# Attention and MoE in one kernel: batch 1's attention in another order, and the last output tile by column halves

## Chip, cores, metric

One core of one Trainium2 chip. The metric is device time in microseconds. The kernel before takes 328.93 us (median of 3 runs, 327.4 to 330.0). With one core there is no other core to compare with, so a run is marked slow here when it is over 1.5% above the fastest of the same kernel. Engines: PE is TensorE (PEld its weight loads), ACT the scalar engine, DVE VectorE, POOL GpSimd, SP the sync engine; a "q" behind the name (SPq) is the engine's sequencer.

## The reference, cut to what matters

```python
# q, k, v: (batch 8, heads 8, seq 576, head_dim 64), f32
scores = q @ k.transpose / sqrt(64)
heads 0..3: mask rel in [0, 32)            # "local"
heads 4..7: mask same position modulo 32   # "strided"
x = softmax(scores) @ v                    # -> (4608 tokens, 512)
h = x @ w_in                               # layer 1: 512 -> 2048
g = where(h > 0, h, exp(min(h, 0)) - 1)
out = g @ w_out                            # layer 2: 2048 -> 512
```

## The kernel before

The order in which each engine works is written by hand; every engine takes its own queue in order. Tokens go through the MoE in 18 groups of 256; `l2` is a quarter of a layer 2 tile (four matmuls of 512 columns, 0.87 us), used as filler for TensorE wherever attention leaves it waiting. While batch 1's attention runs, a string of tokens says what stands next: "2" one layer 2 step, S scores, A or B the product P v (A in a two-bank PSUM tile, B in two one-bank tiles), E the normalisation, T transposes, "a" casts of K and V, "c" the cast of K's second half, "v" loads of batch 2's V, "k" and "x" further loads, "t" transposes of batch 2. The tiles that the timelines name: `sc` scores, `pm` the masked weights, `so` or `o_ps` with `s_ps` the product P v and its sums, `ln` and `rc` the normalisation, `tp` transposes, `xT` attention's output as layer 1 reads it, `hps` layer 1, `ops` and `opl` layer 2, `osb` the output tile in SBUF, `qlb` and `klb` the local heads' Q and K in bf16, `vlx` and `vs` the V of the local and of the strided heads.

```python
p_x = tile_pool("ps_x", bufs=2)   # PSUM, two banks each: scores, A, transposes
p_h = tile_pool("ps_h", bufs=3)   # PSUM, one bank each: layer 1, B
p_o = tile_pool("ps_o", bufs=1)   # PSUM, one bank: layer 2
...
def load_vl16(b):
    for h in range(HG):           # two loads for each of 4 heads
        ...
        nc.gpsimd.dma_start(out=t[PRE:128], in_=x)
        nc.gpsimd.dma_start(out=t[0:PRE, 1:], in_=...)
...
for it in ("2 S4 2 S5 2 2 B4 S6 2 E4 A5 S7 2 E5 B6 a 2 E6 A7 2 E7 v "
           "T0 2 S0 S1 c 2 T1 k B0 2 E0 S2 2 A1 E1 S3 2 B2 E2 2 A3 2 E3 t 2 x").split():
    if it == "2":
        l2_to(l2n[0] + 1)
    elif it == "v":
        load_str(2, vs, v)        # one load, into vs
        load_vl16(2)              # eight loads, into vlx
    elif it == "a":
        cast_k(nc.gpsimd, 0)      # klb, read by T0
        for a in range(2):
            cast_v(nc.gpsimd, 1, a)
    elif it == "c":
        cast_k(nc.scalar, 1)      # klb, read by T1
    ...
for n, (j, t) in enumerate(L1S):  # the main loop
    ...
    l2_to(n + 10)
    ...
    l1(j, t, ...)
```

The last tile's layer 2 is four such steps, one copy by the scalar engine and two stores (56 and 72 rows) by the sync engine.

The softmax here doesn't subtract the row's maximum and nothing guards it: scores larger than these inputs give would overflow.

## Time and profile before

| stage of the profiled run (span 325.9 us) | ends at |
|---|---|
| warm-up, batch 0's attention, first layer 1 | last 16 layer 1 matmuls start at 38.58 us |
| batch 1's attention with 16 layer 2 steps | 65.23 us |
| main loop | last layer 1 group starts at 314.73 us |
| last layer 2 matmul | 321.82 us |
| last copy | 322.44 us |
| end | 325.9 us |

TensorE sets the time in all of them but the end. A row of the timeline reads: start, length (us), engine, line, what it writes and reads, how many; in brackets how long the engine stood idle ahead of it and what released it. At the start of the main loop, TensorE in the kernel before:

```profile
69.97 0.31 PE L359 MATMUL so<-pm,ones 72*64 72x288 bf16 x2 [0.37 <-DVE pm L289]
71.57 0.31 PE L359 MATMUL so<-pm,ones 72*64 72x288 bf16 x2 [1.16 <-DVE pm L289]
72.94 0.30 PE L284 MATMUL sc<-qsT,ksT 64*128 64x72 bf16 x8
```

Two P v products wait 1.53 us together for VectorE. At the end, the DMA activity from 320 to 326 us in 40 slices of 0.15 us (tenths busy, then GB/s):

```profile
DMA  4767862100000000000002578868520000000000
GB/s 150 232 177 205 287 219 96 41 0 0 0 0 0 0 0 0 0 0 0 0 0 96 205 205 246 259 205 246 150 109 27 0 0 0 0 0 0 0 0 0
```

The last tile's data move in slices 21 to 30, 323.15 to 324.65 us; 1.25 us pass from there to the end.

### The profile page before, as it was taken

To read this page: it belongs to the slowest core of one execution; us is meant where nothing else is said; L and a number is where in the kernel's file an instruction comes from. 1 tells how busy PE (TensorE), PEld (TensorE's weight loads), DVE (VectorE), ACT (ScalarE), POOL (GpSimd) and SP (SyncE) were. 2 spreads that over 40 slices of the span, in tenths; PEclk is the share of its full clock that TensorE was granted. 3 is DMA by queue.
4 is the path that set the end of the run, shared out by engine and by line. 5 is a ranking of instruction groups with operands and counts; after the bars stand their busy time and mean duration, and the time that the engine had idled before them with its cause. 6 is when DMAs were issued, how large, how long until landed. Compare 5 with 4: busy or idle time off the path is not lost.

```text
span 325.9 us, 7664 instructions
## 1 busy us (share of the span) xinstructions
PE 309.4 (95%) x2933; PEld 222.6 (68%) x2976; DVE 246.0 (75%) x481; ACT 221.0 (68%) x429; POOL 101.2 (31%) x121
## 2 busy tenths in 40 slices
PE   8899997989999989999999999989999999999994
PEld 6669944566667767767777677757777777777762
DVE  6764973467778898898888988998888866666660
ACT  3798765687778877777778777877877734444431
POOL 6262414962672445263245443540000000000000
PEclk9999999999999999999999999999999999999999
DMA  8999999999799939992999299939111111111212
GB/s 165 192 207 209 221 185 151 141 193 184 114 126 214 202 87 146 224 183 68 132 224 217 70 144 232 174 92 162 48 45 37 34 34 32 33 34 44 55 32 64
DMA packets 55179, 41.98 MB, mean 129 GB/s; under 512 B 38296, under 2 KB 45784, under 8 KB 55144
## 3 DMA queue, kind: packets, MB, share of 16 engines
q0 software_dynamic: 21040, 24.49, 45.7%
q1 hardware_dynamic: 32780, 16.42, 24.6%
q10 hardware_dynamic: 1324, 0.59, 0.8%
q8 instruction: 23, 0.38, 0.5%
q14 instruction: 12, 0.10, 0.1%
HBM read 38.18 MB, written 9.44 MB: 146 GB/s over the span
## 4 chain that ended last, share of the span: by engine, by line
PE 74%; DVE 13%; ACT 5%; issue 4%; DMA 3%; POOL 0%; DVEq 0%; ACTq 0%
PE ops L454 32%; PE hps L397 30%; DVE g L412 3%; PE ox L336 3%; PE sc L284 3%; DVE he L411 3%; DMA ks<-in_k_dram 3%; DVE xT L304 2%; PE idle L464 1%; DVE pm L295 1%; DVE g L431 1%; PE hpw L422 1%; DVE xT L308 1%; PE tp L261 1%; PE o_ps L369 1%
## 5 line engine op out<-in xcount | busy, mean ns | idle before, releaser
L454 PE MATMUL ops<-w_out_sb,g 128*128 128x512 bf16 x533 | 140.5, 380 | 2.7 <-issue 0.8
L397 PE MATMUL hps<-xT,w_in_sb 128*128 128x256 bf16 x1088 | 140.7, 273 | 0.6 <-DVE g L412 0.4
L397 PEld LDWEIGHTS <-w_in_sb 128*128 128x128 bf16 x1088 | 117.4, 114 | 22.7 <-issue 0.6
L404 ACT ACTIVATE he<-hps 128x512 f32<-128x512 f32 x136 | 80.2, 593 | 53.7 <-PE hps L397 52.7
L412 DVE TENSOR_TENSOR g<-he,hps 128x512 bf16<-128x512 bf16 x130 | 89.4, 687 | 13.5
L454 PEld LDWEIGHTS <-g 128*128 128x128 bf16 x576 | 52.0, 98 | 39.1 <-DVE g L412 0.3
L411 DVE TENSOR_SCALAR he<-he 128x512 bf16<-128x512 f32 x130 | 59.9, 461 | 20.5 <-ACT he L404 19.1
L287 ACT ACTIVATE e<-sc 128x576 bf16<-128x576 f32 (+1 forms) x64 | 38.6, 645 | 4.5 <-PE sc L284 4.4
L459 ACT COPY osb<-ops 128x512 f32<-128x512 f32 x36 | 21.1, 587 | 15.5 <-PE ops L454 13.2
L339 ACT ACTIVATE ln<-ox 64x288 f32<-64x288 f32 x40 | 16.3, 409 | 12.3 <-PE ox L336 11.7
L304 DVE TENSOR_TENSOR xT<-ox,rc 64x288 bf16<-64x288 f32 x40 | 18.1, 453 | 5.0 <-ACT rc L342 4.7
L308 DVE TENSOR_TENSOR xT<-ox,rc 64x288 bf16<-64x288 f32 x40 | 18.1, 453 | 4.0 <-ACT rc L342 3.7
L295 DVE TENSOR_TENSOR pm<-e,mask_l 128x576 bf16<-128x576 bf16 x32 | 17.9, 591 | 3.3 <-ACT e L287 3.0
L150 POOL COPY vsx<-vs 72x1024 bf16<-72x1024 bf16 x10 | 11.2, 1146 | 23.9 <-DMA vs<-in_v_dram 18.8
L342 ACT ACTIVATE rc<-ln 128x288 f32<-128x288 f32 x40 | 17.7, 443 | 1.3
L289 DVE TENSOR_TENSOR pm<-e,mask_s 72x576 bf16<-72x576 bf16 x32 | 16.0, 527 | 2.5 <-ACT e L287 2.2
L340 ACT ACTIVATE ln<-ox 64x288 f32<-64x288 f32 x40 | 16.1, 402 | 0.5
L464 PE MATMUL idle<-warm 128*128 128x256 bf16 x92 | 15.1, 312 | 1.3 <-DVE warm L173 1.3
L144 POOL CAST vlx<-vl 128x768 bf16<-128x768 f32 x13 | 10.6, 843 | 17.6 <-DMA vl<-in_v_dram 16.6
L138 POOL CAST klb<-kl 96x768 bf16<-96x768 f32 x11 | 9.8, 907 | 19.9 <-DMA kl<-in_k_dram 14.8
L129 POOL DMA_DIRECT2D qs<-in_q_dram x8 | 6.5, 806 | 29.9 <-DMA qsT<-qs 25.2
L135 POOL CAST qlb<-ql 72x1024 bf16<-72x1024 f32 x10 | 11.6, 1186 | 3.8 <-DMA ql<-in_q_dram 3.8
(98 smaller groups left out, 256.4 us busy)
## 6 DMA issues: line engine op xcount, KB each, us to landing
out_dram<-osb SPq DMA_DIRECT2D x32, 144.0 KB
vl<-in_v_dram POOLq DMA_DIRECT2D x7, 576.0 KB, 17.8
kl<-in_k_dram POOLq DMA_DIRECT2D x6, 576.0 KB, 14.6
ql<-in_q_dram POOLq DMA_DIRECT2D x5, 576.0 KB, 15.7
qs<-in_q_dram POOLq DMA_DIRECT2D x8, 288.0 KB, 7.4
ks<-in_k_dram POOLq DMA_DIRECT2D x8, 288.0 KB, 9.7
vs<-in_v_dram POOLq DMA_DIRECT2D x8, 288.0 KB, 9.7
w_in_sb<-in_moe_w_in_dram POOLq DMA_DIRECT2D x2, 1024.0 KB, 16.3
```

The costliest lines, as they stand in the source:

```text
L287: nc.scalar.activation(e[0:R], sc[0:R, :, 0:W], ACT.Exp, scale=scale)
L295: nc.vector.tensor_mul(pm, e, mb.unsqueeze(1).to_broadcast([128, 2, W]))
L304: nc.vector.tensor_mul(xs[:, u * W:(u + 1) * W], o[pr], rc[pr])
L308: nc.vector.tensor_mul(dst, o[pr].rearrange(pat, b=3, s=NS), rc[pr].rearrange(pat, b=3, s=NS))
L342: nc.scalar.activation(rc, ln, ACT.Exp, scale=-1.0)
L397: nc.tensor.matmul(hps[:, mm], lhsT=w_in_of(m, c), rhs=xT[:, c, r0:r0 + SUB], start=(c == 0), stop=(c == KC - 1))
L404: nc.scalar.activation(e, hps, ACT.Exp)
L411: eng.tensor_scalar(e1, e, scalar1=1.0, scalar2=1.0, op0=ALU.min, op1=ALU.subtract)
L412: nc.vector.tensor_tensor(gt, e1, hps, op=ALU.max)
L454: nc.tensor.matmul(ops, lhsT=g[:, m, kk * 128:(kk + 1) * 128], rhs=w_out_sb[:, m, :], start=(m == 0), stop=(m == MC - 1))
L459: nc.scalar.copy(o_sb, ops)
L464: nc.tensor.matmul(ps, lhsT=warm[:, 0:128], rhs=warm[:, 0:ps.shape[-1]], start=True, stop=True, skip_group_check=True)
```

## The change

Its intent: join the visits to the scores, put every P v of batch 1 in one-bank tiles so that they do not compete with the scores, move three layer 2 steps into the main loop's first iterations where TensorE waits, and let the last tile's copy and store start sooner and on two engines. On the way "v" came to stand ahead of "a", both K casts went to GpSimd, and the second copy of the first transposes (T0) went from the scalar engine to VectorE. The cut below leaves out the lines of the function `l2_to` that now call `l2_last` for the last tile.

```diff
-    def store(c0, o_sb):
+    def store(c0, o_sb, cols=slice(0, 512), engs=(nc.sync,)):
 ...
+            engs[i % len(engs)].dma_start(out=out_v[b, s, p:p + n, cols],
+                                          in_=o_sb[c - c0:c - c0 + n, cols])
+    def l2_last(j, kk):
+        for i in range(2):
+            ops = p_h.tile([128, n], F32, tag="h", name="opl")     # n = 256
+            for m in range(MC):
+                nc.tensor.matmul(ops, lhsT=..., rhs=w_out_sb[:, m, i * n:(i + 1) * n], ...)
+            nc.scalar.copy(o_sb[:, i * n:i * n + n // 2], ops[:, 0:n // 2])
+            nc.vector.tensor_copy(o_sb[:, i * n + n // 2:(i + 1) * n], ops[:, n // 2:])
+            store(j * SUB + kk * 128, o_sb, slice(i * n, (i + 1) * n), (nc.sync, nc.scalar))
 ...
-    for it in ("2 S4 2 S5 2 2 B4 S6 2 E4 A5 S7 2 E5 B6 a 2 E6 A7 2 E7 v "
-               "T0 2 S0 S1 c 2 T1 k B0 2 E0 S2 2 A1 E1 S3 2 B2 E2 2 A3 2 E3 t 2 x").split():
+    for it in ("2 S4 S5 2 2 B4 S6 S7 E4 2 B5 2 E5 B6 2 E6 B7 2 E7 v a "
+               "T0 2 S0 S1 2 T1 k B0 2 E0 S2 S3 B1 2 E1 B2 2 E2 B3 2 E3 t x").split():
 ...
         elif it == "a":
-            cast_k(nc.gpsimd, 0)
+            for a in range(2):
+                cast_k(nc.gpsimd, a)
             for a in range(2):
                 cast_v(nc.gpsimd, 1, a)
-        elif it == "c":
-            cast_k(nc.scalar, 1)
 ...
-            piece_T(1, n, (nc.vector, nc.scalar))
+            piece_T(1, n, (nc.vector, nc.scalar if n else nc.vector))
 ...
-        l2_to(n + 10)
+        l2_to(max(n + 10, min(n + 13, 16)))
```

More of the change, by code (lines that the diff above doesn't have):

```diff
@@ L434 @@
     out_v = out.rearrange("(b p s) f -> b s p f", b=B, s=NS)
-    def store(c0, o_sb):
-        c = c0
+    def store(c0, o_sb, cols=slice(0, 512), engs=(nc.sync,)):
+        c, i = c0, 0
         while c < c0 + 128:
@@ L441, in store @@
             n = min(RS - p, c0 + 128 - c)
-            nc.sync.dma_start(out=out_v[b, s, p:p + n, :],
-                              in_=o_sb[c - c0:c - c0 + n, :])
-            c += n
+            engs[i % len(engs)].dma_start(out=out_v[b, s, p:p + n, cols],
+                                          in_=o_sb[c - c0:c - c0 + n, cols])
+            c, i = c + n, i + 1
     acc = {}
@@ L460, in l2 @@
             store(j * SUB + kk * 128, o_sb)
+    def l2_last(j, kk):
+        g, n = g_of[j], d_model // 2
+        o_sb = p_wk.tile([128, d_model], F32, tag="osb", name="osb")
+        for i in range(2):
+            ops = p_h.tile([128, n], F32, tag="h", name="opl")
+            for m in range(MC):
+                nc.tensor.matmul(ops, lhsT=g[:, m, kk * 128:(kk + 1) * 128],
+                                 rhs=w_out_sb[:, m, i * n:(i + 1) * n],
+                                 start=(m == 0), stop=(m == MC - 1))
+            nc.scalar.copy(o_sb[:, i * n:i * n + n // 2], ops[:, 0:n // 2])
+            nc.vector.tensor_copy(o_sb[:, i * n + n // 2:(i + 1) * n], ops[:, n // 2:])
+            store(j * SUB + kk * 128, o_sb, slice(i * n, (i + 1) * n), (nc.sync, nc.scalar))
     def spin(ps):
@@ L576, in l2_to @@
             j, kk, part = L2S[l2n[0]]
-            late = kk and j == NSUB - 1
-            l2(j, kk, part, *((p_h, "h") if late else (p_o, "o")))
+            if (j, kk) != (NSUB - 1, 1):
+                l2(j, kk, part, p_o, "o")
+            elif part == 0:
+                l2_last(j, kk)
             l2n[0] += 1
-    for it in ("2 S4 2 S5 2 2 B4 S6 2 E4 A5 S7 2 E5 B6 a 2 E6 A7 2 E7 v "
-               "T0 2 S0 S1 c 2 T1 k B0 2 E0 S2 2 A1 E1 S3 2 B2 E2 2 A3 2 E3 t 2 x").split():
+    for it in ("2 S4 S5 2 2 B4 S6 S7 E4 2 B5 2 E5 B6 2 E6 B7 2 E7 v a "
+               "T0 2 S0 S1 2 T1 k B0 2 E0 S2 S3 B1 2 E1 B2 2 E2 B3 2 E3 t x").split():
         n = int(it[-1]) if it[-1].isdigit() else 0
```

## The prediction

> **What bounds the kernel now.** I first read the chain that ended last, to know which engine sets the end; then the timelines of TensorE and GpSimd around batch 1's attention, where most of the change lies; then the last microseconds. TensorE holds three quarters of the chain:
>
> ```profile
> PE 74%; DVE 13%; ACT 5%; issue 4%; DMA 3%; POOL 0%; DVEq 0%; ACTq 0%
> ```
>
> So what counts is how long TensorE's in-order queue takes through each stage. In the busy times by stretch, 40 to 65.2 us is batch 1's attention, filled up with layer 2 steps, and 65.2 to 78.2 us the start of the main loop (columns: stretch, length, then busy us of PE, PEld, DVE, ACT, POOL; clock, DMA share, GB/s):
>
> ```profile
> 50.60:57.00 6.40, 4.42 (x74) 2.61 (x75) 2.19 (x5) 3.93 (x8) 3.79 (x6) 1.00 0.88 158
> 57.00:65.20 8.20, 7.97 (x90) 4.27 (x91) 4.04 (x10) 5.47 (x12) 7.94 (x12) 1.00 1.55 141
> 65.20:78.20 13.00, 11.31 (x142) 8.96 (x141) 9.50 (x19) 11.35 (x23) 5.59 (x7) 1.00 1.05 192
> ```
>
> TensorE is idle 2.0 us in the first and 1.7 us in the last, where scalar engine and VectorE are behind and no layer 2 filler stands in the queue. Those are the gaps that the author is after. GpSimd looks harmless in the chain (0%), but its order of work is the key to my prediction:
>
> ```profile
> 46.57 0.82 POOL L138 CAST klb<-kl 96x768 bf16<-96x768 f32 x1 [6.15 <-DMA kl<-in_k_dram]
> 53.21 1.59 POOL L144 CAST vlx<-vl 128x768 bf16<-128x768 f32 x2 [5.82 <-DMA vl<-in_v_dram]
> 54.75 0.72 POOL L129 DMA_DIRECT2D vs<-in_v_dram  x1
> 55.45 0.75 POOL L125 DMA_DIRECT2D vlx<-in_v_dram  x1
> ...
> 60.22 0.59 POOL L126 DMA_DIRECT2D vlx<-in_v_dram  x1
> 61.06 2.89 POOL L117 DMA_DIRECT2D klb<-in_k_dram  x4 [0.24 <-PE o_ps L369]
> ```
>
> Here the cast of K's first half (klb) is done at 47.4 us, 3.6 us before TensorE wants it for batch 1's transposes. The nine V loads come after the casts and hold GpSimd for 6.1 us, 54.75 to 60.81. TensorE takes klb at 51.02:
>
> ```profile
> 51.02 0.43 PE L261 MATMUL tp<-identity,klb 96*128 96x96 bf16 x6
> 65.23 1.91 PE L397 MATMUL hps<-xT,w_in_sb 128*128 128x256 bf16 x16
> ```
>
> **What the Trainium skill says.** (1) "DMA: Bandwidth & Descriptors", section "SWDGE vs HWDGE vs iDMA": descriptors of a DMA issued from GpSimd are computed by its own cores. The trace agrees: each such issue is a GpSimd row of 0.59 to 1.22 us, and the next row starts as it ends. (2) "TensorE: Matmul & The Clock Gate", Part 1: after an idle window of about 3.4 us the array falls to half rate, and needs as long of activity to come back. The trace's start agrees: the first 26 warm-up matmuls of 256 columns took 5.47 us, 0.21 us each, against 0.109 us later (8 of L397 in 0.87 us). (3) "PSUM — Partial Sum Buffer", section "PSUM bank collisions raise a hardware error": two engines may not read one bank's quadrant at once. I found no row of the trace before that tests it; in the build of the changed kernel VectorE's copy of each last half waits for the scalar engine's, so the two copies do not overlap.
>
> **The change part by part.**
>
> 1. *GpSimd's order.* The new order puts "a" (casts of K and V) behind "v" (loads of batch 2's V), and gives it both K casts; before, K's second half was cast on the scalar engine. In the build's order of GpSimd's instructions, the nine loads now stand ahead of the four casts. The first load overwrites vs, so it waits for the last P v product of batch 1's strided heads (B7). The others wait too: the build cycles eight semaphores, so each GpSimd load waits for the landing of the one eight before it. The trace before shows such a stall:
>
> ```profile
> 30.46 0.74 POOL L113 DMA_DIRECT2D qlb<-in_q_dram  x1 [0.28 <-DMA qs<-in_q_dram]
> ```
>
> The eight before qlb was qs, issued at 19.38 and landed 10.8 us later, at 30.2. By this count the sixth vlx load waits for batch 2's qs, the seventh for ks, the eighth for vs. The DMA view of the issues at 39.6 to 40 us (last column: us from issue to landing) gives two of them:
>
> ```profile
> qs<-in_q_dram POOLq DMA_DIRECT2D x1, 288.0 KB, 16.4
> ks<-in_k_dram POOLq DMA_DIRECT2D x1, 288.0 KB, 18.0
> ```
>
> Issued at 38.78 and 39.69 they land at 55.2 and 57.7. vs, issued at 54.75, took 5.2 us: 59.95. Issued earlier it still stands behind ks in the queue, and ks to vs is 2.25 us, about what qs to ks took (2.5), so the queue's rate sets it: I keep 59.95. Then: B7 near 50.9, five vlx loads done by 55.2, the seventh at 57.7, the eighth at 60.0 plus 0.6, the cast 0.82: **klb ready at 61.4 us, against 47.4**. TensorE reaches the transposes at about 52.3 (below) and stands for 9 us.
>
> 2. *Joint visits and one-bank tiles before that point.* Scores S4,S5 and S6,S7 now stand together. B4 still waits for VectorE's first pm (44.79 in the trace), since VectorE works off layer 1 until 44.3. With two e's more ahead of it on the scalar engine, the first ln ends at 47.2, not 46.5, and B5, which reuses the bank of B4's sums (three banks in that pool), waits for it; the copy of the finished layer 2 tile moves behind too. I make it B7 at 50.5 to 50.9, transposes at 52.3, before 50.6. This slips about 1.5 us but vanishes in the 9 us wait.
>
> 3. *From klb to the main loop.* Work that remains for TensorE: klb transposes 0.36, six layer 2 steps of 0.97 (5.8), scores 0.36 + 0.4, T1 0.75, four P v at 0.37 (1.5), last transposes 1.18: 10.35 us. Waits that the three-bank pool and the scalar engine's order bring (first e after the tile copy 0.3, B2 on ln 0.4, B3 on the copy and ln 1.0): 1.35. The clock: after 9 us idle the array is cold; the start of the trace says about 5.3 us at half rate, in which 2 to 2.5 us are lost; I take 2.2. Sum 13.9: main loop at 61.4 + 13.9 = 75.3, against 65.23: **+10.0 us**.
>
> 4. *Three layer 2 steps moved.* They are already left out above (six instead of eight remain after T0). In the main loop they add 3 x 0.87 = 2.6 us of work, but TensorE stood 0.37 + 1.16 us there for pm, and the scalar engine catches up meanwhile. Followed through, the second P v ends 7.7 us after the loop's start, not 6.8: **+0.9 us**.
>
> 5. *The end.* Before: the last matmul ends at 321.83, then
>
> ```profile
> 321.85 0.59 ACT L459 COPY osb<-ops 128x512 f32<-128x512 f32 x1 [2.87 <-PE ops L454]
> ```
>
> and two stores of 2 KB rows, whose data move from about 323.0 to 324.65; the rest to 325.9 is completion. After: 32 matmuls of 256 columns at 0.109, 3.47 us as with 16 at 0.217. The copies of the second half, 128 columns each, one behind the other: scalar engine 0.27 (1.02 us for 1024 columns and 0.59 for 512 give 0.83 ns per column and 0.17 fixed), VectorE an estimated 0.25 from its 0.46 for 288: 0.55, nothing saved. Half the bytes: 0.6 us saved. Two engines issue at once: 0.3 saved. **-0.9 us.**
>
> Sum: +10.0 + 0.9 - 0.9 = +10.0 us on 328.93, about 338.9; I say **338.5 us**.
>
> **The rivals.**
> - *The intent holds*: filler goes where the gaps are, 1.5 to 2 us of gaps close, the end gains 0.9, about 326 us. For it: the gaps are there. Against: it needs klb at 52 us, and the build puts nine GpSimd loads first, the first of them behind B7. Even with every landing early, 50.9 + 6.1 + 0.8 is 57.8.
> - *Only the issue time counts*: vs and ks land early or the order of semaphores is not as I count. Then klb at about 58, 3.4 us less, and 335 us.
> - *No cold clock*: some activity (the q transposes) keeps the array awake, or the ramp falls in waits: 2.2 us less, 336.5 us.
> - *More than I count*: the loads of V, earlier in the queue, slow ks, or the cold stretch is longer: 341 us.
>
> **Range and chances.** The 2% line is 335.5 us. A stop of TensorE of 5.5 us at least seems sure, so faster is very unlikely (0.02). The second and third rivals together would bring about 333, within 2%: 0.18. Slower: 0.80. Range 333.0 to 342.0.
>
> **What would show it.** In the changed kernel: GpSimd's klb cast behind nine load rows, ending near 61 us; TensorE idle about 9 us before the klb transposes, put down to GpSimd or to a landing; the layer 2 groups after it at 1.7 us rather than 0.97; the first layer 1 group of the main loop near 75 us; no waits for pm at the first two P v of the loop; from 85 us on the same pattern as before, shifted; from last matmul to end 3.2 us instead of 4.1. If klb is cast before 53 us, my main step is wrong and the kernel gets faster; if the gap is 5 us, the landings were mis-sized; if the groups after it take 0.97, the clock was.

## The result

The changed kernel takes 338.32 us (median of 3 runs, 337.67 to 340.65) against 328.93: slower, ratio 1.031 (95% interval 1.021 to 1.041). Ratios here are the mean time of one kernel's fast runs over that of the other's of the same rounds, so not quite the ratio of the medians that I quote. The profiled run has a span of 336.6 us, 10.7 more than before. The chain of waits:

```profile
PE 65%; DVE 10%; ACT 3%; issue 3%; DMA 1%; SPq 0%; DVEq 0%
```

GpSimd is not in that list. But the shares add up to 82% only, where those of before add up to 99%: followed back from the end, the chain stops at 60.6 us, 18% of the span from its start, at the klb transposes. A chain that doesn't reach the start is worth a look at the place where it stops. The timelines show what is there. First GpSimd in the changed kernel:

```profile
51.62 0.71 POOL L129 DMA_DIRECT2D vs<-in_v_dram  x1 [10.60 <-PE o_ps L369]
...
56.19 0.61 POOL L126 DMA_DIRECT2D vlx<-in_v_dram  x1 [0.49 <-issue]
58.06 0.74 POOL L125 DMA_DIRECT2D vlx<-in_v_dram  x1 [1.26 <-DMA ks<-in_k_dram]
59.20 0.59 POOL L126 DMA_DIRECT2D vlx<-in_v_dram  x1 [0.40 <-DMA vs<-in_v_dram]
59.79 1.60 POOL L138 CAST klb<-kl 96x768 bf16<-96x768 f32 x2
```

The first load waits 10.6 us for the P v that reads vs; the last two wait for the landings of ks and vs; only then comes the cast whose input had been there for 12 us. TensorE in the same kernel:

```profile
52.22 0.45 PE L259 MATMUL tp<-identity,qlb 72*64 72x72 bf16 x16
60.68 0.66 PE L261 MATMUL tp<-identity,klb 96*128 96x96 bf16 x6 [8.01 <-POOL klb L138]
61.56 1.49 PE L454 MATMUL ops<-w_out_sb,g 128*128 128x512 bf16 x3 [0.22 <-issue]
...
66.41 0.81 PE L454 MATMUL ops<-w_out_sb,g 128*128 128x512 bf16 x3 [0.16 <-issue]
...
73.70 1.04 PE L397 MATMUL hps<-xT,w_in_sb 128*128 128x256 bf16 x8
```

It stands for 8.01 us. The layer 2 group right after it takes 1.49 us for three matmuls, a group of the same form five microseconds later 0.81: the first ran at half clock. The busy times by stretch (the column after POOL's is the granted clock):

```profile
54.00:56.00 2.00, 0.00 (x0) 0.00 (x0) 0.00 (x0) 0.00 (x0) 1.71 (x3) 0.57 1.19 228
62.00:64.00 2.00, 1.92 (x16) 0.80 (x15) 0.20 (x1) 0.91 (x2) 2.00 (x4) 0.50 0.00 0
64.00:66.00 2.00, 2.00 (x32) 1.07 (x31) 1.00 (x3) 0.77 (x2) 0.34 (x1) 0.87 1.03 106
```

A mean of 0.57 over two microseconds is half clock for 1.72 of them, so the clock fell at 54.28; by the same sum on the last line it came back at 64.52 (the trace's own clock record has 54.30 and 64.54). That is 10.24 us of half clock, of which TensorE had work from 60.68 on.

At the main loop's start, the waits for VectorE's pm are gone, and another has come:

```profile
80.88 0.31 PE L359 MATMUL so<-pm,ones 72*64 72x288 bf16 x2
81.00 0.32 PE L369 MATMUL so<-pm,vs 72*64 72x72 bf16 x8
83.10 0.31 PE L284 MATMUL sc<-qsT,ksT 64*128 64x72 bf16 x8 [0.78 <-DVE xT L304]
```

The scores at 83.10 wait for a two-bank PSUM tile until VectorE has taken the P v before from it. And the end:

```profile
330.87 0.27 ACT L472 COPY osb<-opl 128x128 f32<-128x128 f32 x1 [1.16 <-PE opl L469]
...
332.62 0.27 ACT L472 COPY osb<-opl 128x128 f32<-128x128 f32 x1 [1.48 <-PE opl L469]
332.92 0.29 DVE L473 COPY osb<-opl 128x128 f32<-128x128 f32 x1 [1.45 <-ACT osb L472]
333.24 0.34 ACTq L442 DMA_DIRECT2D out_dram<-osb  x1
```

The second half's last copy ends at 333.21 us, the span at 336.6: 3.4 us, as before (3.46). The sum of the profiled runs, changed against before:

| stretch | before, us | changed, us | difference |
|---|---|---|---|
| to the last 16 layer 1 matmuls (same code) | 38.58 | 39.16 | +0.58 |
| from there to the main loop | 26.65 | 34.54 | +7.89 |
| to the scores after the second P v (72.94; 83.10) | 7.71 | 9.40 | +1.69 |
| to the last layer 1 group (314.73; 325.46) | 241.79 | 242.36 | +0.57 |
| to the last matmul (321.82; 332.59) | 7.09 | 7.13 | +0.04 |
| to the end | 4.08 | 4.01 | -0.07 |
| sum | 325.9 | 336.6 | +10.7 |

From those scores to the last matmul the 14 profiles take 248.2 to 250.7 us, so a microsecond more or less there in one profile is scatter.

### The profile page after: what moved, and what is told of

The parts are those of the page before. It is cut to its first block, busy times and chain, and to the rows that moved or that the text cites. A ratio compares the mean times of both kernels' runs of the same rounds, so it can differ in the third digit from the quotient of the medians.

```text
span 336.6 us, 7703 instructions
## 1 busy us (share of the span) xinstructions
PE 311.5 (93%) x2948; PEld 225.0 (67%) x2992; DVE 248.0 (74%) x484; ACT 219.4 (65%) x428; POOL 102.1 (30%) x122
## 4 chain that ended last, share of the span: by engine, by line
PE 65%; DVE 10%; ACT 3%; issue 3%; DMA 1%; SPq 0%; DVEq 0%
PE ops L454 28%; PE hps L397 27%; PE ox L336 3%; DVE he L411 3%; DVE g L412 3%; PE sc L284 2%; DVE xT L304 2%; DMA ksT<-ks 1%; DVE xT L308 1%; PE opl L469 1%; PE tp L261 1%; ACT rc L342 1%; ACT ln L340 0%; ACT ln L339 0%; DVE pm L295 0%
## 5 line engine op out<-in xcount | busy, mean ns | idle before, releaser
L454 PE MATMUL ops<-w_out_sb,g 128*128 128x512 bf16 x516 | 137.9, 382 | 3.4 <-issue 0.9
L411 DVE TENSOR_SCALAR he<-he 128x512 bf16<-128x512 f32 x130 | 63.7, 490 | 21.8 <-ACT he L404 20.4
L454 PEld LDWEIGHTS <-g 128*128 128x128 bf16 x560 | 50.8, 98 | 38.4 <-issue 1.7
L295 DVE TENSOR_TENSOR pm<-e,mask_l 128x576 bf16<-128x576 bf16 x32 | 15.4, 512 | 3.6 <-ACT e L287 3.3
L289 DVE TENSOR_TENSOR pm<-e,mask_s 72x576 bf16<-72x576 bf16 x32 | 15.2, 502 | 2.2 <-ACT e L287 1.9
L129 POOL DMA_DIRECT2D vs<-in_v_dram x8 | 6.1, 768 | 22.9 <-PE so L369 12.3
```

The lines of the kernel that those rows point to most:

```text
L411: eng.tensor_scalar(e1, e, scalar1=1.0, scalar2=1.0, op0=ALU.min, op1=ALU.subtract)
L454: nc.tensor.matmul(ops, lhsT=g[:, m, kk * 128:(kk + 1) * 128], rhs=w_out_sb[:, m, :], start=(m == 0), stop=(m == MC - 1))
```

## The experiments

My theory: GpSimd's order (the nine loads ahead of the casts) is the whole loss, through the wait and the clock that falls in it; the moved steps cost in the loop about what they save ahead of it; the end saves nothing. The rivals: the author's intent, which would show as soon as the order is mended; and the joint visits or the pool of three banks as a cause of their own. "Before" in each group of runs is the kernel before on the same chip. All kernels gave the right result.

**1. The changed kernel with the casts first.**

```diff
- "... 2 E6 B7 2 E7 v a T0 ..."
+ "... 2 E6 B7 2 E7 a v T0 ..."
```

> The changed kernel with one swap: the casts of K and V are put ahead of the nine V loads on GpSimd again, all else as changed. My theory (GpSimd's order is the whole loss): klb is cast by 47 to 48 us, TensorE goes through the transposes at about 52.3 us without a stop, stays warm, and the main loop starts at 52.3 + 11.7 = 64 us, or at most 65 (73.70 in the changed kernel, 65.23 before). With about 1.7 us for the three moved steps (0.9 at the second P v, 0.8 at the wait for the scores' bank that follows) and nothing saved at the end, 328.5 to 330 us, level with before. Rival A (the author's intent, once the order is mended): the gaps close and the end gains, 326 to 327 us. Rival B (the joint visits and the three-bank pool cost as much as the order): it stays above 333 us.

Measured: 329.07 us (6 runs) against 327.22, ratio 1.0046 (1.0012 to 1.0079). TensorE in its profile:

```profile
52.16 0.45 PE L259 MATMUL tp<-identity,qlb 72*64 72x72 bf16 x16
52.55 0.43 PE L261 MATMUL tp<-identity,klb 96*128 96x96 bf16 x6
...
64.11 1.04 PE L397 MATMUL hps<-xT,w_in_sb 128*128 128x256 bf16 x8
```

No stop, and 11.56 us from klb to the main loop where the changed kernel took 13.02. One swap of two tokens takes back 9.3 us of medians (338.32 to 329.07; 2.6% by the ratios), so Rival B falls. So does Rival A: what is left of the change is not faster than before but some 1.5 us slower, a little more than "level". In this profile batch 1's attention is 1.66 us shorter (24.99 against 26.65), the loop's start takes those back (the wait of 0.78 us for xT is there, at 73.51), and between there and the last matmul the profile takes 1.86 us more than before, 1.08 of them at one wait for VectorE at 91.53. The changed kernel's two profiles, with the same program in the loop, have no such wait and differ from before by +0.61 and -0.57 us there, so the 1.86 us are within the scatter. Where the 1.5 us of the times lie stays open.

**2. The kernel before with the loads first.**

```diff
- "... 2 E5 B6 a 2 E6 A7 2 E7 v T0 ..."
+ "... 2 E5 B6 2 E6 A7 2 E7 v a T0 ..."
```

> The kernel before with one move: the casts of K's first half and of V are put behind the nine V loads on GpSimd, all else as before (K's second half stays on the scalar engine). My theory: TensorE stands 8 to 9 us ahead of the klb transposes, goes cold, and the time is +8 to +9.5 us, 336.5 to 339 us. Rival B: the order alone is worth less than half of the loss, under 333 us.

Measured: 337.92 us (4 runs) against 327.22, ratio 1.0314 (1.0277 to 1.0351): the whole loss, by the order alone, in a kernel that has nothing else of the change.

```profile
60.45 0.66 PE L261 MATMUL tp<-identity,klb 96*128 96x96 bf16 x6 [9.67 <-POOL klb L138]
```

**3. The casts between the two halves of the loads.**

```diff
- "... 2 E7 v a T0 ..."          # v: vs and eight vlx loads
+ "... 2 E7 v a V T0 ..."        # v: vs and four vlx loads; V: the other four
```

> The changed kernel with the casts between the two halves of the loads: vs and four vlx loads, then the four casts, then four vlx loads. The three loads that wait for the landings of qs, ks and vs then stand behind the casts. My theory (issue time plus waits for landings): klb is cast at about 55.0 + 0.8 = 55.8 us instead of 60.6, TensorE idle 3.3 us rather than 8, the main loop 4.8 us earlier plus what the cold clock cost (up to 1.4): 332 to 333.8 us. Rival (the waits for landings are harmless, only the nine issues count): each load skipped saves 0.7 us, four of them 2.7 us, klb at 57.9 us, about 335.6 us.

Measured: 335.27 us (4 runs: 335.45, 336.18, 335.08, 331.0; the second marked slow) against 327.22, ratio 1.0191 (1.013 to 1.0253), which at the 2% line is unclear. The median is above what my theory said, and near what its rival said; but the profile shows that the agreement with the rival is an accident:

```profile
55.88 0.66 PE L261 MATMUL tp<-identity,klb 96*128 96x96 bf16 x6 [3.19 <-POOL klb L138]
56.34 1.91 PE L454 MATMUL ops<-w_out_sb,g 128*128 128x512 bf16 x4
...
62.55 1.89 PE L454 MATMUL ops<-w_out_sb,g 128*128 128x512 bf16 x4
```

klb comes at 55.88, as worked out from issue times and landings (55.8), and not at 57.9. But the layer 2 steps after it stay at half speed for far longer than in the changed kernel, and the main loop starts at 71.09, 15.21 us after klb rather than 11.56. The clock in this kernel, by stretch:

```profile
54.00:56.00 2.00, 0.12 (x2) 0.13 (x3) 0.00 (x0) 0.00 (x0) 2.00 (x4) 0.81 1.18 230
...
64.00:66.00 2.00, 2.00 (x24) 1.11 (x23) 0.90 (x2) 1.17 (x3) 2.00 (x3) 0.63 1.54 91
```

It fell at 55.24 and came back at 65.48: again 10.24 us, though TensorE had work again 0.64 us after the fall. The shorter wait let more work lie in the half clock: 3.65 us lost where the changed kernel lost 1.46.

**4. Warm-up matmuls in the changed kernel's wait.**

```diff
+ for _ in range(3):                       # ahead of T0
+     hot = p_h.tile([128, 256], F32, tag="h", name="hot")
+     for _ in range(19):
+         spin(hot)                        # a matmul nobody reads
```

> The changed kernel with 57 warm-up matmuls of 256 columns (about 6.2 us) put in TensorE's queue ahead of the transposes, so that it works through most of its wait for klb. If the clock goes cold in the wait and costs 1.3 us or so afterwards: the first layer 2 step after the wait takes 0.97 us rather than 1.5, klb's transposes start at the same time (60.7), and the kernel is 1 to 1.6 us faster, 336.7 to 337.3 us beside 338.3. If the idle clock costs nothing: the same within 0.3 us. If the extra matmuls run past klb's cast: slower.

Measured: 336.5 us (6 runs) against 327.22, ratio 1.0279 (1.0243 to 1.0316).

```profile
60.50 0.43 PE L261 MATMUL tp<-identity,klb 96*128 96x96 bf16 x6 [1.64 <-POOL klb L138]
...
72.06 1.04 PE L397 MATMUL hps<-xT,w_in_sb 128*128 128x256 bf16 x8
```

klb comes at the same time, the clock stays at 1.00 throughout, and klb to main loop is 11.56 us, exactly as with the casts first. The half clock cost the difference, 1.46 us.

**5. The split loads with warm-up matmuls**, as experiment 3 with three times nine such matmuls ahead of T0.

> The kernel with the casts between the two halves of the loads, and 27 warm-up matmuls (2.9 us) in TensorE's 3.2 us wait for klb. In the kernel without them klb came when expected (transposes at 55.88 us), but the clock stood at a half from 55.2 to 65.5 us, and the way from the transposes to the main loop took 15.2 us instead of 11.56. If that half clock is why it came out 2 to 3 us slower than expected: the clock stays whole, the main loop starts at 55.9 + 11.6 = 67.5 us (71.09 without), and the time is 3 to 3.6 us less, 331.5 to 332.5 us. If something else held it: 334 us or more.

Measured: 331.54 us (4 runs) against 328.37, ratio 1.0104 (1.0065 to 1.0143).

```profile
55.17 0.43 PE L261 MATMUL tp<-identity,klb 96*128 96x96 bf16 x6 [0.27 <-POOL klb L138]
...
66.73 1.04 PE L397 MATMUL hps<-xT,w_in_sb 128*128 128x256 bf16 x8
```

Again 11.56 us, and 3.7 us of medians less than without them (0.9% by the ratios, 2.9 us), as expected. So the half clock, and not the count of landings, was what experiment 3 missed. That its fourth run took 331.0 us fits this: it has no trace, but its mean granted clock, 0.995, leaves room for 3.3 us of half clock, where the profiled run's 0.982 stands for 12 (10.24, and some more after the last matmul).

**6. The changed kernel again**, on the chip of the experiments, for the comparison with 4.

> The changed kernel itself on the same chip as the experiments, for the comparison with the kernel with warm-up matmuls in the wait. Its clock stood at a half from 54.3 to 64.5 us; the half clock overlapped TensorE's work for 3.8 us and cost 13.02 - 11.56 = 1.46 us. Expected 337.5 to 339 us, 1 to 2 us above the kernel with the warm-up matmuls (336.5); if it is within 0.5 us of that one, the half clock was not worth what the trace says.

Measured: 338.79 us (6 runs) against 328.37, ratio 1.0325 (1.0297 to 1.0352). By ratios the warm-up matmuls are worth 0.46%, 1.5 us. In this profile klb comes at 61.59 and the main loop at 75.26: klb differs by about a microsecond between the two profiles. The half clock lasts from 56.64 to 66.88, 10.24 us once more, and costs 13.67 - 11.56 = 2.11 us here.

The clock records show what these spells have in common: in each of the 14 traces the changes of the clock lie whole multiples of 3.413 us apart, counted from the first change, which comes 3.95 to 7.30 us after the start of the span. So where the steps fall in batch 1's attention differs from run to run. The spell of three steps is not a rule: experiment 10's profile has one of a single step (72.73 to 76.14), and one of the changed kernel's first three runs has a mean clock of 0.990, which leaves room for some 7 us at most. (Half clock for a run: its span times the missing share of the clock, times two.) What decides the length of a spell stays open: in experiment 3 TensorE was busy for 98% of the spell's middle step, and the clock stayed at half.

**7. The changed end alone**, on the kernel before (`store`, `l2_last` and the function `l2_to` that calls it; the call `l2_to(n + 10)` in the main loop stays as before).

> The kernel before with the changed end alone: last tile by column halves, copied by two engines in turn, stored by two. From the traces of the changed kernel and of the one with the casts first: from the end of the last copy to the end of the span 3.4 us as before (3.46), although the data of the last stores move for 1.0 instead of 1.7 us; the copies end 0.6 us after the last matmul either way. Theory: 0 within 0.3 us of before. The prediction's term: 0.9 us faster.

Measured: 328.45 us (6 runs) against 327.29, ratio 1.001 (0.997 to 1.0051). Last matmul to end: 322.94 to 327.0, 4.06 us; before 4.08.

**8. The same with all stores by the sync engine.**

```diff
- store(..., slice(i * n, (i + 1) * n), (nc.sync, nc.scalar))
+ store(..., slice(i * n, (i + 1) * n))
```

> As the kernel with the changed end alone, but all four stores of the last tile issued by the sync engine. If the second issuing engine is what lengthens the completion (1.7 us from last data to the end, against 1.2 before) and eats what the halved bytes save, this one is 0.3 to 0.6 us faster than before. If it is the halves themselves (1 KB rows, fixed time of a store), it is level with before, or 0.2 to 0.4 us slower than with two engines because the issues queue up.

Measured: 326.88 us (6 runs) against 327.29, ratio 0.9964 (0.9929 to 1.0). Last matmul to end: 321.55 to 325.6, 4.05 us. So the end is nearly the same with one queue, with two, and with no halves, and the 0.36% of the times lies ahead of the last matmul, where this kernel and that of experiment 7 have the same program. I take it for scatter; experiment 11 repeats it. The DMA activity from 317.6 to 325.6 us in 40 slices of 0.2 us:

```profile
DMA  0000000004567762004446200005265100000000
```

The last data have moved by the end of slice 31, at 324.0 us: 1.8 us after the last copy (322.17) and 1.6 us ahead of the end. Before it was 2.2 us after the copy and 1.25 us ahead of the end. So the halved transfer is done sooner, and something after it takes longer. The semaphore records of the packed traces show what, in all 14 profiles alike (landing: the last increment of the semaphores that the last two stores raise):

| last tile | profiles | copy end to landing, us | landing to end, us |
|---|---|---|---|
| whole, one queue | 5 | 2.56 to 2.57 | 0.92 to 0.93 |
| halves, two queues | 7 | 2.04 to 2.06 | 1.34 to 1.36 |
| halves, one queue | 2 | 2.11 | 1.29 to 1.30 |

The landing does come 0.45 us sooner with the halves, and 0.06 us sooner still with the second queue. But the program closes with the sync engine waiting for nine semaphores in a fixed order (114, 100, 103, 104, 105, 115 to 118), some 0.06 us each. The stores of the kernel before end on 117 and 118: seven waits are over before they land, and none is left behind them. With two stores more, the cycle of eight semaphores ends on 100 and 103, and six or seven waits are left when they land (in this run from 324.30 to 324.73). Those 0.4 us eat most of what the halves save; from the last matmul to the end 0.06 to 0.10 us remain. No run here changes which semaphore the last store gets, so that the 0.4 us could be had is not shown.

**9. The three layer 2 steps moved, alone**, on the kernel before.

```diff
- "2 S4 2 S5 ... E0 S2 2 A1 ... E3 t 2 x"
+ "2 S4 S5 ... E0 S2 A1 ... E3 t x"
- l2_to(n + 10)
+ l2_to(max(n + 10, min(n + 13, 16)))
```

> The kernel before with three layer 2 steps taken out of batch 1's attention and put into the first three steps of the main loop, all else as before. The prediction's term: the loop pays 0.9 us for them where they were worth 2.6 in a queue without gaps. What the trace of the casts-first kernel shows: the loop pays 1.7 us (0.8 more at a wait for the scores' bank, 78 lines after the loop's start). Theory: the attention stage gets 1.5 to 2.6 us shorter, the loop 1.7 longer, the time 0 to 0.9 us shorter than before. Rival: the removed steps leave gaps of the same length in the attention stage, which waits for its scalar engine and VectorE: then up to 1.7 us slower.

Measured: 328.34 us (6 runs) against 327.29, ratio 1.002 (0.9979 to 1.0061): level, neither theory nor rival told apart by the time. In the profile the attention stage is 24.67 us, 1.98 shorter than before, and the loop's start is 1.69 longer (63.38 to 72.78, 9.40 us, against 7.71), with the wait for xT at the same place as in the changed kernel:

```profile
72.78 0.31 PE L284 MATMUL sc<-qsT,ksT 64*128 64x72 bf16 x8 [0.78 <-DVE xT L304]
```

**10. The joint visits and one-bank tiles alone**, on the kernel before, casts first, all 16 steps in the attention stage.

```diff
- "2 S4 2 S5 2 2 B4 S6 2 E4 A5 S7 2 E5 B6 a 2 E6 A7 2 E7 v T0 2 S0 S1 c 2 T1 ..."
+ "2 S4 S5 2 2 2 B4 S6 S7 E4 2 B5 2 E5 B6 2 E6 B7 2 E7 a v T0 2 S0 S1 2 T1 ..."
```

> The kernel before with batch 1's scores in joint visits, its P v all in one-bank tiles, both K casts on GpSimd ahead of the loads, and the 16 layer 2 steps all in batch 1's attention. The casts-first kernel's attention stage was 1.65 us shorter than before with three steps (2.6 us) fewer in it, so the visits and the one-bank tiles by themselves cost about 1 us: theory 0.5 to 1.5 us slower than before. Rival (the author's intent): they close waits of TensorE and are worth 1 us or more.

Measured: 328.64 us (6 runs) against 327.29, ratio 1.0023 (0.9982 to 1.0065). The attention stage takes 26.60 us, before 26.65, so in the profile the visits neither save nor cost anything there. The times can't tell: their interval, 0.6 us less to 2.1 us more, holds both 0 and the 1 us that I expected. (The profiled run also has the half clock of one step named under 6, at the loop's start.) I had reckoned the 1 us by taking the three steps that experiment 1 lacks as 2.6 us of its attention stage; experiment 9 shows that taking them out shortens the stage by 1.98 only, since the rest of their time filled waits.

**11. Two attempts at a faster kernel.** First the same three steps as in 9, but placed where the trace shows waits: one ahead of the first P v of the loop, one between the two, one ahead of the next scores.

```diff
- l2_to(max(n + 10, min(n + 13, 16)))
+ l2_to(max(n + 10, min(n + 11, 16)))
```

> The kernel before with the same three layer 2 steps taken out of batch 1's attention, but put where the main loop's start shows waits: one ahead of the first P v, one between the two (1.16 us idle before), one ahead of the next scores (0.78 us idle in the kernel with the steps at the loop's first iterations). Theory: the loop pays about 0.5 to 1 us for them, not 1.7, so TensorE is 1 us ahead of before at the scores that follow, and the time is 0.5 to 1.2 us below before, a quarter of a per cent, hardly above the scatter of the runs. Rival: what is gained at the start is lost again at later waits of the loop for VectorE: level with before.

Measured: 327.19 us (6 runs) against 328.37, ratio 0.9987 (0.9952 to 1.0023).

```profile
69.66 0.31 PE L359 MATMUL so<-pm,ones 72*64 72x288 bf16 x2
...
71.90 0.30 PE L284 MATMUL sc<-qsT,ksT 64*128 64x72 bf16 x8
```

The waits are gone and TensorE is 1.04 us ahead of before at the scores (72.94 there). The loop's start takes 8.74 us, 1.03 more than before, for 2.6 us of added work. At 91.84 nearly all of the lead is spent again, on a wait of 0.98 us for VectorE; by the last matmul this profile is 1.25 us ahead of before (320.57 against 321.82), which is within the scatter of the loop. Then both parts that came out below before, together:

> The two parts that came out below before, together: the three layer 2 steps put into the waits of the main loop's start (ratio 0.9987), and the last tile by column halves with all stores from the sync engine (0.9964). In the traces the end takes 4.05 us from the last matmul with the halves, from one queue or two, and 4.08 before, so the second part should be worth nothing and its 0.9964 be scatter: theory 0.997 to 1.000 of before. If the halves from one queue are really worth 0.36%, 0.995 of before or less.

Measured: 326.66 us (6 runs, 324.95 to 328.08) against 328.08 (327.36 of its fast runs), ratio 0.9974 (0.9927 to 1.0021), and 4.06 us from last matmul to end. That is in the range for "the second part is worth nothing". It is the lowest ratio but one, and its interval holds 1: I can't say that it beats the kernel before. It does beat the changed kernel, by 3%.

## Why the prediction was right, point by point

The time (338.5 predicted, 338.32 and 338.79 measured) and the direction are right, and so is the step that carries them. Two terms of the sum are wrong, and errors of opposite sign helped the total.

1. *GpSimd's order.* Right, but for the sixth vlx load, whose gap of 0.49 us the trace does not put down to qs (the fifth ended 0.3 us after qs had landed). The loads wait for B7, then for ks and vs by the count of eight; klb at 61.4 predicted, 60.68 and 61.59 measured in two profiles. Shown by experiments 1 and 2 from both sides: the swap alone takes the loss away from the changed kernel and puts it into the kernel before. That the landings count, not only the issues, is shown by klb's times with the split loads (55.88 in experiment 3).
2. *Joint visits before that point.* The transposes were reached at 52.22, predicted 52.3, and the waits named (for the first ln, for the tile's copy) are in the trace with 0.23 and 0.63 us. That this "vanishes in the wait" is so.
3. *From klb to the main loop.* 13.9 predicted, 13.02 measured: work and waits 11.56, predicted 11.7; half clock 1.46, predicted 2.2. The 11.7 holds a slip: the three waits listed add up to 1.7 us, not 1.35. The mechanism is right; the size of the half clock is not, because I took it for a ramp that starts when the work resumes. In four profiles it was a spell of 10.24 us that began during the wait, so that a shorter wait can cost more (experiments 3 and 5). The times of passage (2) do not fit these traces, and the measurement decides: the clock fell 1.6 us after TensorE had stopped in the changed kernel (52.67 to 54.30), 2.5 us in experiment 3 and 4.3 us in experiment 6, and at the start of the kernel before it came to full 5.1 us after the first matmul (1.26 to 6.33).
4. *The moved steps.* The term is too small: 0.9 predicted, 1.69 measured (four profiles with the old start at full clock take 7.30 to 7.71 us, seven with the new one 9.39 or 9.40). Up to the second P v the trace agrees (8.47 us behind at the loop's start, 9.31 there). I stopped following there. The next scores then wait 0.78 us for the PSUM tile which VectorE still reads; the filler that closed the first two waits had let TensorE run ahead into the third.
5. *The end.* Wrong: -0.9 predicted, -0.07 measured, and next to 0 in experiments 7, 8 and 11. The copies one behind the other are as predicted (0.27 and 0.29 us; the two terms listed add up to 0.52, not 0.55). The failing step is "Half the bytes: 0.6 us saved. Two engines issue at once: 0.3 saved", with "the rest to 325.9 is completion" taken as a fixed remainder. By the landings of experiment 8 the half bytes saved 0.45 us and the second queue 0.06; the remainder was not fixed, for the closing semaphore waits behind the landing grew from 0.92 to 1.35 us. The Trainium skill, "DMA: Bandwidth & Descriptors", section "Latency and other measured facts", puts most of a DMA's fixed cost of about 2 us down to the receipt from the target memory. It does not explain this: from the end of the last packet to the landing these traces have 0.34 us with the whole tile and 0.34 or 0.35 with the halves.

The rival "no cold clock" is refuted by the granted clock of 0.50; "only the issue time counts" by the waits for ks and vs in the trace. The rival of the intent fell with experiment 1.

Of the total: the stretch to the main loop was taken for 2.1 us too much, the moved steps for 0.8 too little, the end for 0.8 too little, and 1.15 us of the measured difference lie in stretches where the prediction claimed none (0.58 ahead of the change, 0.57 in the rest of the loop). The sum of that is within 0.7 us of what was said (338.5 was itself 0.4 below the prediction's own sum of 338.9, with no reason given), by luck more than by precision.

## What to carry to other kernels

Read each engine's new order by itself, an engine with a 0% share of the chain too: an engine that both casts and issues loads makes a cast wait for whatever the loads ahead of it wait for, here a reader of the buffer and the landings of older loads. When filler is moved to where TensorE waits, put it in front of each wait by name, and follow on to the next wait after it; and a short idle stretch can cost more than a long one when the clock falls just as work returns (3.65 us in experiment 3, 1.46 in the changed kernel). At the end of a kernel, follow the last transfer to its landing and then on to the end: here the halved transfer landed 0.5 us sooner, and the waits behind it took 0.4 back.

## What the Trainium skill lacked or had wrong

- "TensorE: Matmul & The Clock Gate", Part 1: it gives one busy window of about 3.4 us as enough for the full clock. In four profiles the half clock lasted 10.24 us, three such windows; with the split loads TensorE had work from 0.64 us after the fall and still stayed at half for 9.6 us. In a fifth profile it lasted 3.41 us.
- No page has it: the clock record of a trace begins with its first change, 6.33 us after the start in the kernel before. Ahead of it the views print 1.00, while 26 warm-up matmuls of 256 columns took 5.47 us, 0.21 each, twice the later 0.109.
- No page has it: in this build a load issued by GpSimd waits for the landing of the one eight before it, and all work behind it on GpSimd waits too (1.26 us for ks and 0.40 for vs in the changed kernel).
- No page has it: the program's closing waits for DMA semaphores stand one behind the other on the sync engine, some 0.06 us each. Landing to end was 0.92 us with none of them left behind the last landing, and 1.29 to 1.36 with six or seven.
